# Attention's first half: transposes by row tiles of 64 queries, a bank for each

## The chip, the cores and the metric

The kernel runs on one core of a Trainium2 chip. The metric is the time of one execution on the device, in microseconds (us), as the median of several runs. Five engines work side by side, each through its own instructions in order, and semaphores hold one back for another: TensorE (PE: matmuls, with PEld its loads of weights), VectorE (DVE), ScalarE (ACT), GpSimd (POOL) and SyncE (SP, which issues the DMAs). TensorE multiplies a block of weights that was loaded before (the stationary operand) with columns that stream through (the moving operand), and writes only to PSUM, which has eight banks of 512 float32 columns on 128 partitions. TensorE's array can be cut: a matmul with tile shape 64x128 uses 64 of its 128 rows, one with 128x64 uses 64 of its columns, and two such halves can have matmuls of their own. The trace writes this shape with a star (64*128) ahead of the shape of the moving operand.

## What is computed

Attention with a bias from a small network, and then an MLP with squared ReLU over the concatenated heads:

```python
scores = scale * np.matmul(q, k.transpose(0, 1, 3, 2)) + bias   # 4 batches, 8 heads, 576 x 576, float32
scores = scores - np.max(scores, axis=-1, keepdims=True)
attn = np.exp(scores)
attn = attn / (np.sum(attn, axis=-1, keepdims=True) + 1e-09)
attn_out = np.matmul(attn, v)
x = attn_out.transpose(0, 2, 1, 3).reshape(B * S, H * D)         # 2304 x 512
h = np.maximum(x @ w_in, 0.0)                                    # 512 -> 2048
return (h * h) @ w_out
```

## The kernel before

A **unit** is a batch, a pair of heads and a chunk of 128 queries (chunk 4, TAIL, holds the last 64 queries, of both heads of the pair side by side). There are 80 units. Units 0 to 39 (batches 0 and 1, in the order of chunks, TAIL first, so units 0 to 7 are tails) are the first half of attention; there the bias table is made along with the work. Units 40 to 79 are the second half, then comes the MLP. The change touches the first half alone.

**What a unit needs.** Its scores `sp` (L425) are four matmuls, of two heads by two halves of the keys; each has 64 rows (the head's 64 dimensions), and heads lie in different halves of the array's rows. Each float32 matmul appears as two instructions in the trace. DVE adds the bias and finds the maximum (L438), ACT takes the exponential (L445) into `p`, whose partitions are queries and whose 1152 columns are the keys of both heads. For the product with v (`px`, L547) the keys must lie on partitions, so p is transposed in blocks of 128 by 128: eight full blocks, `pp` (L529), four to a bank, and the block of the two heads' last 64 keys, `pa` (L521). A transpose loads the block of p as weights and streams the identity matrix through. A tail unit has four full blocks and pa. ACT copies the banks to `pt` in SBUF (L851 in the first half, L1123 in the second).

**The order of the first half.** From step s = 2 to 39 the order on PE, DVE and ACT is the order in which step(s) writes it. On PE: the scores of unit s; in steps 34 to 38 `rp` (L474), the turned sums of a finished group; the transposes of unit s - 2 (`turned`); one to three blocks of bias sums `bb` (L383, 16 matmuls each; none from step 31 on); the product `px` of unit s - 3; in some steps ra and rt (L490). On ACT a step begins with the copies to pt; behind them come, alternating, the reads of bb (L388) and the exponentials (L445). Of the 30 steps whose transposed unit is full (10 to 39), nine have three blocks bb (10, 12, 14, 18, 20, 22, 26, 28, 30), ten have two (the odd ones from 11 to 29 that are left), two have one (16 and 24) and nine have none (31 to 39).

**Banks.** In the first half pp, pa, bb, px, rp, ra and rt share four PSUM banks (pool aux); sp has the other four. A bank is written again when its readers are done. In the program as it is built, in a step of full units with three bb the second bb is written to the bank of the first pp of the same step, the third to that of the second pp, and px to that of pa. With two bb the second has the bank of the first pp, and px that of the second pp. With one bb, px has the bank of the first pp. With none, px has the bank of an earlier step. This is the same with the change.

Of the kernel before, what the change touches and what calls it, by code (L numbers as in the profile page):

```python
# [10 lines left out]
F32 = mybir.dt.float32  # L11
# [10 lines left out]
B, H, S, D = 4, 8, 576, 64  # L22
# [8 lines left out]
TAIL = 4  # L31
# [9 lines left out]
QB, PB, TB, MB, BB, TL, RB = 3, 3, 2, 4, 3, 2, 1  # L41
# [27 lines left out]
TL = 2  # L69
# [8 lines left out]
def attention_then_relu2_mlp(ctx: ExitStack, tc: tile.TileContext, q, k, v, cols, w_in, w_out, psi, xmat, dist, out):  # L78
    nc = tc.nc
    PE, DVE, ACT, POOL, SP = nc.tensor, nc.vector, nc.scalar, nc.gpsimd, nc.sync  # L80
# [5 lines left out]
    att = att_stack.enter_context(tc.tile_pool(name="att", bufs=1, side="right"))  # L86
# [5 lines left out]
    def bank(name, tag=None):  # L92
        if tag is None:
            return bank_p["p"].tile([128, 512], F32, name=name, tag="aux", bufs=4)
        if tag in held:
            return held.pop(tag)
        return bank_p["p"].tile([128, 512], F32, name=name, tag=tag, bufs=1)
# [10 lines left out]
    ident = att.tile([128, 128], F32, name="ident")  # L108
# [30 lines left out]
    def scale_xc(ic):  # L139
        return ACT.activation(out=xc_t[ic], in_=xc_t[ic], func=AF.Identity, scale=bscale)  # L140
# [3 lines left out]
    units = [(b, hp, ic) for ic in chunks for b in range(AB) for hp in range(HP)]  # L144
# [261 lines left out]
    p_t, pt_t, sum_t = {}, {}, {}  # L406

    def score_products(u, pin=True):
        b, hp, ic = units[u]
        kt, qt = k1_t[b, hp], q_t[b, hp]  # L410
        negm = att.tile([128, 2], F32, name="negm", tag="negm", bufs=3)
        if (b, hp) not in sum_t:
            sum_t[b, hp] = att.tile([128, 9], F32, name="sums", tag="sums", bufs=AB * HP + 2)
        p_t[u] = att.tile([128, 2 * S], F32, name="p", tag="p", bufs=PB)

        nsp = 2 if ic < TAIL else 1
        sp4 = ps.tile([128, 4, 512], F32, name="sp", tag="sp", bufs=1)
        sps = [sp4[:, 2 * n:2 * n + 2] for n in range(nsp)]
        cols = slice(128 * ic, 128 * ic + 128 if ic < TAIL else S)

        for m, (x, h) in enumerate((x, h) for x in range(2) for h in (1, 0)):
            rows = slice(64 * h, 64 * h + 64)
            k0 = HALF * x + (64 if h and ic == TAIL else 0)
            out_t, to = (sps[h], slice(0, 128)) if ic < TAIL else (sps[0], rows)
            mm = PE.matmul(out_t[to, x, :HALF], lhsT=qt[rows, cols], rhs=kt[rows, k0:k0 + HALF], start=True, stop=True)  # L425
            if m and pin:
                tc.keep_in_program_order(mm)
        return negm, sps
# [4 lines left out]
    def reduce(u, n, negm, sp):  # L433
        b, hp, ic = units[u]
        p, sums = p_t[u], sum_t[b, hp]
        bias = bias_t[:, 9 * hp + 2 * ic + n]
        t = att.tile([128, S], F32, name="t", tag="t", bufs=TB)
        DVE.tensor_tensor_reduce(  # L438
            out=t.rearrange("p (x n) -> p x n", x=2), in0=sp[:, :, :HALF],
            in1=bias.rearrange("p (x n) -> p x n", x=2), scale=-0.125, scalar=3.0e38,  # L440
            op0=ALU.add, op1=ALU.min, accum_out=negm[:, n:n + 1],
        )

        def weights():
            ACT.activation(out=p[:, S * n:S * n + S], in_=t, func=AF.Exp, bias=negm[:, n:n + 1], scale=-1.0, accum_out=sums[:, 2 * ic + n:2 * ic + n + 1])  # L445
            if ic == TAIL:
                POOL.tensor_copy(out=p[:, S:S + 64], in_=p[:, S - 64:S])

        return weights
# [3 lines left out]
    def scores(u):  # L453
        negm, sps = begun.pop(u) if u in begun else score_products(u)
        for n, sp in enumerate(sps):
            softmax(u, n, negm, sp)
# [41 lines left out]
    def scale_x(b, hp, rows_t):  # L498
        times_rows(b, hp, *spread_rows(rows_t))

    def transposes(us, tags=None):
        next_tag = iter(tags) if tags else None
        groups = []
        pa = None
        for m, u in enumerate(us):
            p_of = p_t.pop(u)
            pt = att.tile([128, 9, 128], F32, name="pt", tag="pt", bufs=2)
            pt_t[u] = pt
            for h in range(2 if units[u][2] < TAIL else 1):
                groups.append((p_of, pt, h))  # L510
            groups.append((p_of, pt, None, m))
        if len(us) > 1:
            heads = [g for g in groups if g[2] is not None]
            groups = heads[:3] + [g for g in groups if g[2] is None] + heads[3:]
        last = []
        for p, pt, h, *m in groups:
            if h is None:
                if pa is None:
                    pa = bank("pa", "d" if tags and len(us) > 1 else next(next_tag) if tags else None)
                at = slice(128 * m[0], 128 * m[0] + 128)  # L520
                PE.transpose(pa[:, at], p[:, S - 64:S + 64], ident)  # L521
                last.append((pt[:, 8], pa[:, at]))
                if len(last) == len(us):
                    yield from last
            else:
                pp = bank("pp", next(next_tag) if tags else None)
                for c in range(4):
                    k0 = h * (S + 64) + 128 * c
                    PE.transpose(pp[:, 128 * c:128 * c + 128], p[:, k0:k0 + 128], ident)  # L529
                yield pt[:, 4 * h:4 * h + 4], pp.rearrange("p (c m) -> p c m", c=4)  # L530

    px_now = [None]

    def values(us, tag=None):
# [278 lines left out]
    def loads(s):  # L813
        for m, g in enumerate(groups[AB * HP:]):
            if s == max(first[g] - KL, NA - AB * HP + 2 + m):
                load_k(*g)
                load_q(*g)
            if s == max(first[g] - KL + TL + 1, NA - AB * HP + 2 + TL + m):
                load_v(*g)
# [7 lines left out]
    def scan_first(s):  # L827
        n = s - AB * HP * TAIL
        if n == 0:
            prep_stack.close()  # L830
            stage_p["scan"] = scan_stack.enter_context(tc.tile_pool(name="scan", bufs=1, side="left"))
        if 3 <= n < SCANS + 3:
            scan_w(n - 3)
        for k in ((0, 1), *((k,) for k in range(2, SCANS)))[n] if n < SCANS - 1 else ():
            fetch(ins[k], stage_p["scan"].tile([128, 1024], F32, name="raw", tag=f"s{k}", bufs=1))

    rest = theta_steps(128, 512)[2:]
    def step(s, plain=True):
        loads(s)
        if plain:  # L840
            scores(s)
        else:
            negm, sps = score_products(s, False)
            exps = [reduce(s, n, negm, sp) for n, sp in enumerate(sps)]
        if s and rest:
            tc.keep_in_program_order(rest.pop(0)())
        n, r = divmod(s, AB * HP)

        def turned():
            for dst, src in transposes((s - TL,)):  # L850
                ACT.copy(dst, src)  # L851

        if not plain:
            rows_made(s - TL)
            turned()
            inverted(s - 1)
            if s >= AB * HP * TAIL:
                scan_first(s)
        if n < TAIL:
            if r == 7 and n + 2 < NIC:  # L860
                tc.keep_in_program_order(scale_xc(chunks[n + 2]))
            if plain:
                bias_upto(NJB * n + BO[r])
                if s == FREE - 1:
                    mask_upto(done + MB)
            else:

                def then():
                    mask_upto(done + MB + 1)
                    if exps:  # L870
                        exps.pop(0)()

                sum_upto(NJB * n + BO[r], then)
            if r == 1 and n + 2 < NIC:
                load_xc(chunks[n + 2])
        if plain:
            if s >= TL:
                turned()
        else:
            for fn in exps:  # L880
                fn()
        u = s - TL - 1
        if u >= 0:
            for piece in values((u,)):
                keep_values(*piece)
            if u in norm_of:
                b, hp, ic = units[u]
                scale_x(b, hp, norm_of.pop(u))
# [3 lines left out]
    def inverted(u):  # L892
        b, hp, ic = units[u]
        if ends(u) and u < NA - TL - 1:
            t = sum_t.pop((b, hp))
            norm_inverse(t)
            norm_of[u] = norm_parts(t)

    def rows_made(u):
        if u in norm_of:  # L900
            norm_of[u] = norm_copy(norm_rows(norm_of[u]))
# [393 lines left out]
    with tc.manual_schedule():  # L1295
# [3 lines left out]
        for i in range(NI + 1):  # L1299
# [4 lines left out]
            n, P = items[min(i, NI - 1)]  # L1304
# [102 lines left out]
```

## Time and profile before

| | us |
|---|---|
| median of 3 runs (704.44 to 704.92) | 704.8 |
| the profiled execution's own time | 704.63 |
| its span, first to last instruction | 702.8 |
| PE busy | 685.8 |
| DVE busy | 552.5 |
| ACT busy | 471.8 |
| first half, steps 2 to 39 | about 28.7 to 188.7 in the span |

The span is what the profiler saw of the profiled execution; 1.8 us lie around it. Busy time is the union of an engine's instructions. On PE instructions overlap: a matmul is listed from the start of its stream to the end of its result, so the distance from one start to the next, not the listed duration, is what a matmul costs in a row of them. A matmul that waits for its weights is listed from before that wait, and so is longer than the next ones of its kind by just that wait. PEld counts as waiting for a releaser that may have been done long before; the length of the idle time is sure, its cause is a guess of the view.

### The profile page before, as it was taken

What the parts mean: (1) busy time and instruction counts of PE and PEld (TensorE: products, weight loads), DVE (VectorE), ACT (ScalarE), POOL (GpSimd) and SP (SyncE); (2) the same over time, 40 slices, a digit from 0 to 9 for tenths busy, and PEclk for the clock granted to TensorE, in tenths of its full rate; (3) what the DMA queues carried; (4) which work ended last, traced back from release to release, by engine and by line L of the source; (5) the groups of instructions that cost most, each with busy time, mean ns of one, the idle gap of its engine ahead of it and who ended that gap; (6) DMA issues with size and microseconds to landing.
All of it is one profiled execution on the core that took longest, in us unless ns stands there. A gap on an engine that the chain in (4) does not pass through costs nothing.

```text
span 702.8 us, 17399 instructions
## 1 busy us (share of the span) xinstructions
PE 685.8 (98%) x6966; PEld 568.7 (81%) x6966; DVE 552.5 (79%) x1165; ACT 471.8 (67%) x952; POOL 196.4 (28%) x313
## 2 busy tenths in 40 slices
PE   7899999999999999999999999999999999999997
PEld 6688888887877877778788888888888888888886
DVE  8999888875788899998898969868477775477664
ACT  5678877878786999998656757676466554446221
POOL 6465544451120355462321403212011112001000
PEclk9999999999999999999999999999999999999999
DMA  6640000007557124410811433060047232633101
GB/s 192 199 134 3 19 2 2 2 3 227 184 206 239 53 68 134 106 31 32 323 67 62 151 144 141 1 226 1 1 151 300 99 110 106 224 120 121 62 1 31
DMA packets 31680, 75.13 MB, mean 107 GB/s; under 512 B 5616, under 2 KB 13936, under 8 KB 30576
## 3 DMA queue, kind: packets, MB, share of 16 engines
q1 hardware_dynamic: 31440, 73.76, 31.1%
q8 instruction: 55, 0.90, 0.5%
q14 instruction: 25, 0.20, 0.1%
q10 hardware_dynamic: 160, 0.26, 0.1%
HBM read 55.66 MB, written 18.35 MB: 105 GB/s over the span
## 4 chain that ended last, share of the span: by engine, by line
PE 87%; DVE 8%; ACT 2%; issue 1%; POOL 1%; DMA 0%; ACTq 0%; POOLq 0%; DVEq 0%
PE y L1284 28%; PE ha L1192 13%; PE sp L425 11%; PE px L547 11%; PE hb L1192 10%; PE pp L529 8%; PE bb L383 5%; DVE t L438 2%; DVE mask L373 1%; ACT pt L1123 1%; PE pa L521 1%; ACT p L445 1%; DVE bt L391 1%; DVE xT L496 0%; PE ra L490 0%
## 5 line engine op out<-in xcount | busy, mean ns | idle before, releaser
L1192 PEld LDWEIGHTS <-area 128*128 128x128 f16 x1680 | 147.7, 98 | 25.3 <-issue 8.4
L1284 PE MATMUL y<-w,gh 128*128 128x512 f32 x576 | 148.9, 398 | 0.6 <-ACT gh L1228 0.6
L1284 PEld LDWEIGHTS y<-w,gh 128*128 128x128 f32 x576 | 105.1, 188 | 22.2 <-ACT gh L1228 1.3
L438 DVE CUSTOM_DVE_ANT_0 t<-sp,area 128x576 f32<-128x576 f32 x144 | 104.2, 753 | 22.4 <-PE sp L425 11.3
L445 ACT ACTIVATE p<-t,negm 128x576 f32<-128x576 f32 x144 | 113.1, 796 | 2.7 <-DVE negm L438 2.1
L425 PE MATMUL sp<-k,q 64*128 64x288 f32 (+1 forms) x640 | 98.9, 426 | 5.5 <-DVE negm L438 3.9
L547 PE MATMUL px<-pt,v 128*64 128x128 f32 (+1 forms) x1600 | 92.2, 266 | 0.0
L547 PEld LDWEIGHTS px<-pt,v 128*64 128x64 f32 x1600 | 79.2, 137 | 11.5 <-ACT pt L1123 6.4
L1192 PE MATMUL ha<-area 128*128 128x256 f16 (+1 forms) x816 | 85.1, 260 | 0.7 <-DVE c L1209 0.7
L399 POOL TENSOR_TENSOR area<-bt,bt 128x256 f32<-128x256 f32 x72 | 66.0, 921 | 69.1 <-DVE bt L391 67.5
L1284 PE MATMUL y<-w,gl 128*128 128x512 f32 x288 | 79.0, 390 | 0.0
L529 PE MATMUL pp<-ident,p 128*128 128x128 f32 x576 | 78.1, 278 | 0.0
L529 PEld LDWEIGHTS pp<-ident,p 128*128 128x128 f32 x576 | 62.6, 141 | 17.6 <-ACT p L445 7.1
L425 PEld LDWEIGHTS sp<-k,q 64*128 64x128 f32 (+1 forms) x640 | 52.9, 175 | 25.3 <-issue 6.1
L1192 PE MATMUL hb<-area 128*128 128x256 f16 (+1 forms) x612 | 64.7, 260 | 0.0
L1284 PEld LDWEIGHTS y<-w,gl 128*128 128x128 f32 x288 | 54.1, 188 | 12.2 <-DVE gl L1229 0.2
L373 DVE TENSOR_TENSOR mask<-sdist,theta 128x1024 f16<-128x1024 f16 x81 | 57.9, 719 | 2.5 <-PE bb L383 0.4
L851 ACT COPY pt<-pp 128x512 f32<-128x512 f32 x68 | 36.9, 589 | 32.3 <-PE pp L529 32.3
L383 PE MATMUL bb<-wmov,mask 128*128 128x64 f16 x1296 | 47.0, 197 | 3.8 <-DVE mask L373 3.7
L1123 ACT COPY pt<-pp 128x512 f32<-128x512 f32 x76 | 41.4, 602 | 13.5 <-PE pp L529 13.3
L383 PEld LDWEIGHTS <-mask 128*128 128x128 f16 x1296 | 44.9, 101 | 6.1 <-DVE mask L373 5.5
L1229 DVE TENSOR_TENSOR gl<-area,gh 128x512 fp32r<-128x512 f32 (+1 forms) x40 | 25.3, 668 | 27.3 <-ACT gh L1228 25.5
(160 smaller groups left out, 992.3 us busy)
## 6 DMA issues: line engine op xcount, KB each, us to landing
raw<-in_w_in SPq DMA_DIRECT2D x32, 512.0 KB, 4.3
r<-in_w_out SPq DMA_DIRECT2D x16, 512.0 KB, 5.7
xs<-area SPq DMA_DIRECT2D x4, 1792.0 KB, 10.9
py<-o SPq DMA_DIRECT2D x12, 512.0 KB, 2.9
o<-py SPq DMA_DIRECT2D x12, 512.0 KB, 4.2
v<-in_v SPq DMA_DIRECT2D x16, 320.0 KB, 3.9
q<-in_q SPq DMA_DIRECT2D x32, 128.0 KB, 3.3
out<-o SPq DMA_DIRECT2D x8, 512.0 KB, 2.9
```

The costliest lines, as they stand in the source:

```text
L373: DVE.tensor_tensor(out=out, in0=win, in1=th, op=ALU.is_ge)
L383: PE.matmul(bb[:, 64 * (7 - r):64 * (8 - r)], lhsT=m[:, r], rhs=wmov[:, n], start=(n == 0), stop=(n == 1))
L399: POOL.tensor_tensor(out=dst, in0=tw, in1=sw, op=ALU.add)
L425: mm = PE.matmul(out_t[to, x, :HALF], lhsT=qt[rows, cols], rhs=kt[rows, k0:k0 + HALF], start=True, stop=True)
L438: DVE.tensor_tensor_reduce(out=t.rearrange("p (x n) -> p x n", x=2), in0=sp[:, :, :HALF], in1=bias.rearrange("p (x n) -> p x n", x=2), sca ...
L445: ACT.activation(out=p[:, S * n:S * n + S], in_=t, func=AF.Exp, bias=negm[:, n:n + 1], scale=-1.0, accum_out=sums[:, 2 * ic + n:2 * ic + n ...
L529: PE.transpose(pp[:, 128 * c:128 * c + 128], p[:, k0:k0 + 128], ident)
L547: PE.matmul(px[64 * h:64 * h + 64, 128 * m:128 * m + w], lhsT=vt[:, c, h], rhs=src, start=(c == 0), stop=(c == 4))
L851: ACT.copy(dst, src)
L1123: ACT.copy(*c)
L1192: PE.matmul(h[:, s, :w], lhsT=a, rhs=x, start=(k == 0), stop=(k == 5))
L1284: PE.matmul(y_t[n][k], lhsT=(gl if m == 2 else gh)[:, slot, o:o + 128], rhs=wl if m == 1 else wh, start=((n, P) in firsts and f == 0 and m ...
```

## The change

In the first half `turned` calls a new generator, `transposes_by_rows`, in place of `transposes`; the second half keeps the old one. The new one takes each full block of p in two halves of 64 queries. Half x has the rows 64x to 64x + 63 of p as weights (64 rows, 128 columns, tile shape 64x128) and 64 columns of the identity as moving operand. The halves alternate: block 0 half 0, block 0 half 1, block 1 half 0, and so on. Each half has a PSUM bank of its own, in which its eight pieces of 64 columns lie one behind the other. So a full unit has 16 matmuls of 64 columns for 8 of 128, and a tail unit 8 for 4. Each bank still has one copy to pt, now 8 runs of 64 (4 runs in a tail unit, which now has two copies in place of one). The last block pa is transposed whole, as before, behind the others; it is asked for when both copies of pp are written down.

```diff
+    def half_block(dst, p, x, k0):
+        rows = slice(64 * x, 64 * x + 64)
+        PE.transpose(dst, p[rows, k0:k0 + 128], ident[rows, rows])
+
+    def transposes_by_rows(u):
+        p = p_t.pop(u)
+        pt = pt_t[u] = att.tile([128, 9, 128], F32, name="pt", tag="pt", bufs=2)
+        n = 8 if units[u][2] < TAIL else 4
+        pp = [bank("pp") for x in range(2)]
+        for c in range(n):
+            for x in range(2):
+                half_block(pp[x][:, 64 * c:64 * c + 64], p, x, c // 4 * (S + 64) + c % 4 * 128)
+        for x in range(2):
+            yield pt[:, :n, 64 * x:64 * x + 64], pp[x][:, :64 * n].rearrange("p (c m) -> p c m", c=n)
+        pa = bank("pa")[:, :128]
+        PE.transpose(pa, p[:, S - 64:S + 64], ident)
+        yield pt[:, 8], pa
@@
         def turned():
-            for dst, src in transposes((s - TL,)):
+            for dst, src in transposes_by_rows(s - TL):
                 ACT.copy(dst, src)
```

Two places show it. On PE, at step 34, the first step that has rp: scores sp, the turned sums rp, transposes pp and pa, product px, and the next step's scores. Before:

```order
L425 MATMUL sp<-k_443,q_446 128x288 x4
L474 LDWEIGHTS parts
L474 MATMUL rp<-ident_b,parts 128x128
L529 MATMUL pp<-ident,p 128x128 x8
L521 MATMUL pa<-ident,p 128x128
L547 MATMUL px<-pt,v 64x128 x10
```

With the change:

```order
L425 MATMUL sp<-k_443,q_446 128x288 x4
L474 LDWEIGHTS parts
L474 MATMUL rp<-ident_b,parts 128x128
L534 MATMUL pp<-ident,p 128x64 x16
L547 MATMUL pa<-ident,p 128x128
L565 MATMUL px<-pt,v 64x128 x10
```

The places in the row are the same; between rp and pa, both with the whole array, there now stand 16 matmuls in halves of its rows.

On ACT, in a step of the bias phase: copies to pt, then reads of bb (to bt) and exponentials (to p) in turn. Before:

```order
L388 ACTIVATE bt_1632<-bb,small 128x256
L851 COPY pt<-pp 128x512 x2
L851 COPY pt<-pa 128x128
L388 ACTIVATE bt_1695<-bb,small 128x256
L445 ACTIVATE p,sums<-t,negm 128x576
```

With the change:

```order
L388 ACTIVATE bt_1704<-bb,small 128x256
L869 COPY pt<-pp 128x8x64 x2
L869 COPY pt<-pa 128x128
L388 ACTIVATE bt_1775<-bb,small 128x256
L445 ACTIVATE p,sums<-t,negm 128x576
```

Number and order of the copies are the same; the first copy used to wait for the fourth matmul of pp of eight, and now waits for the fifteenth of sixteen.

## Rows read from the trace of the kernel before

**Rows 1.** The page: span, busy time of the engines, PE and its clock in 40 slices.
```profile
span 702.8 us, 17399 instructions
PE 685.8 (98%) x6966; PEld 568.7 (81%) x6966; DVE 552.5 (79%) x1165; ACT 471.8 (67%) x952; POOL 196.4 (28%) x313
PE   7899999999999999999999999999999999999997
PEclk9999999999999999999999999999999999999999
```

**Rows 2.** Chain that ended last, 60 to 80 us: start, length, engine, tile, line.
```profile
by line: PE bb L383 26.7%; PE pp L529 25.6%; PE sp L425 23.4%; PE px L547 22.3%; PE pa L521 2.7%
...
67.61 1.17 PE sp L425 x8
68.78 1.02 PE pp L529 x8
69.81 0.11 PE pa L521
69.92 1.40 PE bb L383 x48
71.32 1.24 PE px L547 x20
```

**Rows 3.** Waits of ACT, 60 to 190 us: total, times, longest.
```profile
ACT pt L851 <- PE pp L529: 23.9, 30, 1.1
```

**Rows 4.** Timeline of PE, steps without bb: start, length, instruction, tile shape, count.
```profile
156.29 0.41 PE L425 MATMUL sp<-k,q 64*128 64x288 f32 x2
156.63 1.09 PE L529 MATMUL pp<-ident,p 128*128 128x128 f32 x8
157.56 0.27 PE L521 MATMUL pa<-ident,p 128*128 128x128 f32 x1
157.77 1.31 PE L547 MATMUL px<-pt,v 128*64 128x128 f32 x20
159.01 1.24 PE L425 MATMUL sp<-k,q 64*128 64x288 f32 x8
```

**Rows 5.** Timeline of PEld: first weight loads of pp, of sp, of px.
```profile
160.18 0.14 PEld L529 LDWEIGHTS pp<-ident,p 128*128 128x128 f32 x1 [0.38 <-ACT p L445]
160.24 0.14 PEld L529 LDWEIGHTS pp<-ident,p 128*128 128x128 f32 x1
159.01 0.18 PEld L425 LDWEIGHTS sp<-k,q 64*128 64x128 f32 x1 [0.17 <-issue]
159.12 0.19 PEld L425 LDWEIGHTS sp<-k,q 64*128 64x128 f32 x2
36.32 0.13 PEld L547 LDWEIGHTS px<-pt,v 128*64 128x64 f32 x1
36.38 0.20 PEld L547 LDWEIGHTS px<-pt,v 128*64 128x64 f32 x4
```

**Rows 6.** Timeline of PE, a step of tails (px moves 64 columns).
```profile
36.32 0.80 PE L547 MATMUL px<-pt,v 128*64 128x64 f32 x20
37.05 1.19 PE L425 MATMUL sp<-k,q 64*64 64x288 f32 x8
38.17 0.65 PE L529 MATMUL pp<-ident,p 128*128 128x128 f32 x4
38.66 0.27 PE L521 MATMUL pa<-ident,p 128*128 128x128 f32 x1
```

**Rows 7.** Timeline of PE, a step with rp.
```profile
174.66 0.23 PE L474 MATMUL rp<-ident_b,parts 128*128 128x128 bf16 x1
174.72 1.04 PE L529 MATMUL pp<-ident,p 128*128 128x128 f32 x8
175.60 0.27 PE L521 MATMUL pa<-ident,p 128*128 128x128 f32 x1
```

**Rows 8.** Timeline of PE and ACT, a step with three bb.
```profile
78.14 1.09 PE L529 MATMUL pp<-ident,p 128*128 128x128 f32 x8
79.07 0.27 PE L521 MATMUL pa<-ident,p 128*128 128x128 f32 x1
79.18 1.56 PE L383 MATMUL bb<-wmov,mask 128*128 128x64 f16 x48
80.67 1.31 PE L547 MATMUL px<-pt,v 128*64 128x128 f32 x20
...
78.83 0.58 ACT L851 COPY pt<-pp 128x512 f32<-128x512 f32 x1 [0.99 <-PE pp L529]
79.31 0.59 ACT L851 COPY pt<-pp 128x512 f32<-128x512 f32 x1
79.79 0.28 ACT L851 COPY pt<-pa 128x128 f32<-128x128 f32 x1
```

**Rows 9.** Timeline in the MLP: a wait that ACT ends, ACT's row and PEld's.
```profile
341.16 0.62 ACT L1228 CAST gh<-c 128x512 fp32r<-128x512 f32 x1
...
341.83 0.19 PEld L1284 LDWEIGHTS y<-w,gh 128*128 128x128 f32 x1 [0.87 <-ACT gh L1228]
```

## The prediction

> **What bounds the kernel now.** I read the page first: PE is busy 98% of the span, at full clock throughout (2.4 GHz), and in the first half its slices read 9 [rows 1]. The chain of waits then shows that in this stretch PE alone is the path: sp, pp, pa, bb, px follow each other with nothing of another engine between them [rows 2]. ACT on the other hand waits for pp in each of the 30 steps with full units, 23.9 us in all, 0.80 a step [rows 3]. So a change of the first half is worth what it does to PE's row, and ACT has about 0.8 us a step to give before it counts. What follows the first half starts with PE too, so a shift of PE's row at step 39 is taken to reach the end one to one.
>
> PE's row has to be read from start to start. Three prices come out of it.
>
> *Steady cost.* Eight full transposes last 1.09 [rows 4]. The last one's own latency is 0.27 (pa, alone, has that) and the first waits 0.06 for its weights, so seven distances make 0.76: **0.109 a block**.
>
> *Loads.* With the whole array the second load of pp starts 0.06 after the first: by then the first matmul has its weights and the buffer behind it is free. With half the rows (sp) the third load, the second of its half, starts 0.11 after the first, though it too has 128 columns. With half the columns (px) and 64 columns it is 0.06 [rows 5]. So a load into half the array costs twice as much per column: **0.106** for 64 rows by 128 columns (0.05 for 64 columns). The two halves load side by side, since the fourth load starts with the third.
>
> *Change of shape.* From px in a tail step to sp: 20 matmuls in ten pairs last 0.80, the last start is 0.80 - 0.22 = 0.58 behind the first, at 36.90, and the next load starts at 37.05: 0.15, of which the pair streams 0.053 (64 columns) and 0.10 goes to the change [rows 6]. From sp to pp the last start is at 159.01 + 1.24 - 0.40 = 159.85, and pp's load starts at 160.18: 0.33, again 0.24 of stream and 0.09 to 0.10 [rows 4, 5]. Nothing is loaded ahead across a change, so the load comes on top.
>
> **The change part by part.**
>
> *A pair of halves, steadily.* The trace has no row-tiled transpose. The nearest row is px in a tail step, where two halves of the array alternate with 64 float32 columns each, just as here; there a pair costs (0.80 - 0.22 - 0.05)/9 = 0.059 [rows 6], which is its load of 0.053 plus 0.006, and the stream is hidden in that. Here the stream is the same and the load is 0.106, so a pair costs 0.106 + 0.006 = **0.112**, the two halves side by side. Bounds: 0.058 if the load came as fast as px's, and 0.165 if a half's load and stream (0.106 + 0.053) couldn't overlap. I take 0.112, since the load's time is read from the very shape that is used. So streaming half as many columns gains nothing: a block costs 0.112 where it cost 0.109.
>
> *A full step's PE row.* Before, from the last pair of sp at 156.29 to pa at 157.56: 1.27 (0.33 + 0.06 + 7 x 0.109 + 0.109 = 1.26) [rows 4]. Now sp and pp have one shape, 64x128, so pp's first load hides behind sp's last stream, and the first pair comes 0.24 later; seven pairs more, 0.78; then the change to the whole array for pa, 0.15, and its load, 0.06. Sum 1.23. **-0.03 a full step**: one change of shape is saved before pp and one is bought behind it.
>
> *The first copy starts later.* It needs 15 of 16 matmuls. In the step of [rows 8] the fourth pp started at 78.14 + 0.38 = 78.52, and the copy 0.31 later, at 78.83. Now the first pair starts at 78.14 - 0.09 = 78.05, the last at 78.83, its result comes 0.22 later (the latency of a 64-column matmul) and the copy 0.03 after that, at 79.09: 0.26 later than before. ACT's idle 0.8 covers that for ACT, but not for PE. The copy ends 0.59 later, at 79.68, and frees the bank of the second bb; from the end of an ACT instruction to the load that it releases takes 0.05 (341.78 to 341.83) [rows 9]. The second bb thus can't start before 79.73; before it stood at 79.18 + 0.47 = 79.65 (16 of 48 in 1.56), with the bank free since 79.41. **+0.08**. The second copy ends 0.48 behind the first, at 80.16, so the third bb starts at 80.21, before 80.11: **+0.10**, and px, whose bank (pa's) is free by then, follows it. A new wait of PE thus stands in 19 steps: +0.10 in the nine with three bb, +0.08 in the ten with two: 0.90 + 0.80 = **+1.7**. With one bb px needs the first copy, at 79.73 against 78.14 + 1.60: nothing within 0.01 (two steps). Without bb: -0.03 each in steps 31, 32, 33 and 39: **-0.1**.
>
> *Steps 34 to 38.* Here rp, with the whole array, stands between sp and pp. Before, rp to pa took 175.60 - 174.66 = 0.94 and rp to pp 0.07 [rows 7]. Now two changes come in where there was none: 0.15 and a load of 0.106 to the first pair, seven pairs 0.78, 0.15 and 0.06 to pa: 1.25. **+0.30 each, +1.5.**
>
> *Tails.* In steps 2 to 7 sp has the shape 64x64 [rows 6], so the change ahead of pp may stay: 0.33 + 0.11, three pairs 0.34, 0.21, together 0.98; before from 37.84 to 38.66, 0.82. +0.16, six times: **+1.0**. No row shows two shapes with the same rows and other columns in succession; if that is no change, it is -0.04 as in a full step. I take the change, as every other pair of shapes here pays it. In steps 8 and 9 sp is 64x128: -0.04 each, **-0.1**. The Trainium skill has a rule for this (TensorEngine Tiling (Array Packing), Key Properties): changing the tiling mode, not just the tile, drains TensorE. By it 64x64 to 64x128 is a change as well, and the sum stays; without it the sum is 1.2 less.
>
> *ACT's second copy in tails* (eight more copies of 256 columns): by the copies of 512 and 128 (0.59 and 0.28) about 0.38 each, 0.2 a step more, under ACT's idle time. DVE, POOL, SP and the DMAs have the same instructions in the same order.
>
> Sum: 1.7 - 0.1 + 1.5 + 1.0 - 0.1 = **+4.0**. The profiled execution took 704.63 (0.17 below the median), so **708.6**.
>
> **The rivals.**
>
> *A. The halves double the rate (faster).* If the load of a 64x128 half took no longer than its stream, a pair would cost 0.058. A full step gains 0.41 of PE's row; the first copy would start at 78.71 and end at 79.30, so the second bb, at 79.35, gains only 0.29, the third 0.27. Sum: -9 x 0.27 - 10 x 0.29 - 2 x 0.39 (one bb) - 4 x 0.41 - 5 x 0.08 - 0.4 (tails) = -8.6, **696.0**. It decides at a load of 0.11: anything below gains. For it: the pairs of 64 columns in px do run at 0.059. Against it: sp's loads, 0.11, in the very shape. The Trainium skill states it (TensorEngine Tiling (Array Packing), Theoretical Speedup): up to 2x when a dimension is at most 64; by that page this rival would be the forecast, and the loads of sp speak against it.
>
> *B. The banks don't bind and the tails pay no change (no difference).* If ACT's copy frees the bank early enough (it would have to start some 0.12 sooner than I have it), the 19 steps give -0.03 each, -0.6; with tails at -0.04 (-0.3 for all eight) and rp's +1.5, less 0.2 for the other steps, the sum is +0.4, **705.0**. One of the two alone gives 706.3 or 707.4. For it: the listed end of a copy need not be the moment of its release. Against it: the slack before is only 0.24.
>
> *C. No overlap of load and stream in a half (slower still).* With 0.165 a pair a step without bb loses 0.34, the copies come 0.63 later and the steps with bb lose 0.46: 19 x 0.46 + 0.7 + 1.4 + 5 x 0.67 + 6 x 0.31 + 0.2 = +16, **721**. Against it: sp's pairs, 0.24 apart, are just their stream, so load and stream do overlap in this shape.
>
> That the change doesn't do what it says, the two halves streaming one after the other, would cost 2 x 0.053 = 0.107 a pair, under the load's 0.112: no other time.
>
> **How the numbers follow.** My forecast has 0.71, A 0.10, B 0.14, C 0.05. The range takes in the forecast and B: from 705.0 to the forecast with both open prices at their worse end, the copy in runs of 64 being 0.1 slower (19 x 0.1 = 1.9) and a pair 0.115: 711.0. A and C, 0.15, stay out. About 0.2% (1.4 us) is what a measurement of this kernel can tell from no change; faster than that is A with a little of B, 0.11; slower C and nearly all of the forecast, 0.74; the rest, 0.15, is B.
>
> **What would show it right or wrong.** Right: 16 transposes in about 0.11 + 0.78 + 0.22 of PE's row; no idle PEld ahead of pp but some 0.1 ahead of pa; PE waiting for ACT's copy of pp ahead of the second and third bb in 19 steps; steps of 34 to 38 0.3 longer. Wrong: pairs 0.06 apart (A) or 0.16 (C); bb starting without a wait (B); or a wait somewhere else, for instance of DVE on bt, since ACT's reads of bb come 0.26 later in a step.

## The result, and the profile after

The changed kernel takes **697.21 us** (median of four runs, 696.92 to 697.57), the kernel before 704.62 beside it (704.14 to 704.92): a ratio of **0.9896**, 95% interval 0.9884 to 0.9908. It is faster by 7.4 us, where 708.6 was forecast and 705.0 to 711.0 given as the range. Rival A, with 696.0, came within 1.2 us.

The page of the kernel after says where to look: the span is 7.0 us shorter than in [rows 1] and PE's busy time 9.0 us, at the same mean granted clock (0.997 of full speed in both), while DVE's and ACT's busy times changed by -2.6 and +1.4 us only. So PE's row became shorter, and most of that reached the end. (The page's lines: the span, the busy time of each engine, PE's clock in 40 slices.)

```profile
span 695.8 us, 17950 instructions
PE 676.8 (97%) x7238; PEld 561.5 (81%) x7238; DVE 549.9 (79%) x1165; ACT 473.2 (68%) x960; POOL 196.5 (28%) x313
PEclk9999999999999999999999999999999999999999
```

The step without bb shows the cause bare. The timeline of PE in the kernel after, in a step of the kind of [rows 4] (start, length, line, instruction, tile shape, count):

```profile
156.58 1.24 PE L425 MATMUL sp<-k,q 64*128 64x288 f32 x8
157.66 0.66 PE L534 MATMUL pp<-ident,p 64*128 64x64 f32 x16
158.25 0.33 PE L547 MATMUL pa<-ident,p 128*128 128x128 f32 x1
158.51 1.31 PE L565 MATMUL px<-pt,v 128*64 128x128 f32 x20
159.75 1.24 PE L425 MATMUL sp<-k,q 64*128 64x288 f32 x8
```

Read it from start to start. The last of sp's matmuls starts at 156.58 + 1.24 - 0.40 = 157.42, and the last of pp's at 157.66 + 0.66 - 0.22 = 158.10. Eight pairs stand there, seven distances in 158.10 - 157.66 = 0.44: **a pair of halves costs 0.0625**, where a whole block cost 0.109 and 0.112 was forecast. From the last pair to pa's start are 0.15, the price of the change of shape, as forecast. The weight loads of the same step (PEld) bear out the two statements on shape: the row of pp's loads begins at 157.42, with sp's last matmul, so nothing is drained between sp and pp; pa's load begins at 158.25, behind the change.

```profile
157.42 0.77 PEld L534 LDWEIGHTS pp<-ident,p 64*128 64x128 f32 x16
158.25 0.14 PEld L547 LDWEIGHTS pa<-ident,p 128*128 128x128 f32 x1
```

A step without bb lasts 159.75 - 156.58 = 3.17, against 3.55 before.

A step with three bb, of the kind of [rows 8], on PE and on ACT:

```profile
76.11 1.24 PE L425 MATMUL sp<-k,q 64*128 64x288 f32 x8
77.19 0.66 PE L534 MATMUL pp<-ident,p 64*128 64x64 f32 x16
77.78 0.33 PE L547 MATMUL pa<-ident,p 128*128 128x128 f32 x1
77.94 1.69 PE L383 MATMUL bb<-wmov,mask 128*128 128x64 f16 x48
...
77.89 1.07 ACT L869 COPY pt<-pp 128x512 f32<-128x512 f32 x2 [0.72 <-PE pp L534]
```

Here bb's row lasts 1.69, and 1.56 before [rows 8]: PE stops inside it for 0.13 more than before. That is the wait of the prediction, for the bank that ACT's copy of pp has to free (the run with the short copy, below, shows it), and it takes back a part of the gain: the step is 0.25 shorter (4.70 for 4.95), not 0.38. ACT's waits for pp in the stretch of [rows 3] fell from 23.9 to 18.1 us in total (columns: total, times, longest):

```profile
ACT pt L869 <- PE pp L534: 18.1, 28, 0.8
```

Step by step, from one sp to the next, in the two traces (mean change in us, and what the prediction had; the step lengths are differences of the starts of sp's rows):

| steps | count | forecast each | measured each | measured, all |
|---|---|---|---|---|
| three bb | 9 | +0.10 | -0.23 | -2.06 |
| two bb | 10 | +0.08 | -0.26 | -2.56 |
| one bb | 2 | 0 | -0.36 | -0.71 |
| no bb (31, 32, 33, 39) | 4 | -0.03 | -0.38 | -1.51 |
| rp (34 to 38) | 5 | +0.30 | -0.09 in four, +0.23 in step 34 | -0.13 |
| tails 2, 4, 6, 7 | 4 | +0.16 | -0.04 to -0.06 | -0.18 |
| tails 3 and 5 | 2 | +0.16 | +0.60, +0.38 | +0.98 |
| tails 8, 9 | 2 | -0.04 | -0.18, -0.20 | -0.38 |

The sum is -6.55; ahead of step 2 another 0.3 goes, and 0.3 in step 40. Of these 7.2 the span keeps 7.0: the shift at the end of the first half reaches the end almost one to one.

Two places went the other way. In tail step 3 the first bb waits; in the same step before it followed pa at once, 0.11 behind it. The timelines of PE and of DVE there:

```profile
34.33 0.46 PE L534 MATMUL pp<-ident,p 64*128 64x64 f32 x8
34.72 0.33 PE L547 MATMUL pa<-ident,p 128*128 128x128 f32 x1
35.53 1.09 PE L383 MATMUL bb<-wmov,mask 128*128 128x64 f16 x32 [0.48 <-DVE bt L391]
...
35.07 0.41 DVE L391 TENSOR_TENSOR bt<-bb,xc 128x256 f32<-128x256 f32 x1
```

DVE reads the last bb of the step before until 35.48, and bb starts 0.05 later: a tail step now takes three of the four banks for its transposes instead of two, so that, by the order in which the kernel asks for them, its first bb has the bank of that read, where before its second bb had it.

That this read comes so late in this execution is not the row tiles' doing. PE had been idle for 2.24 us ahead of step 2, and then the granted clock fell to 0.50, its lower level of 1.2 GHz. In this execution it fell inside sp's row, which lasted 2.10, and DVE waited 0.59 for it (PE's and DVE's timelines, and the stretch from 29 to 30 us with the clock behind the five busy times):

```profile
28.44 2.10 PE L425 MATMUL sp<-k,q 64*64 64x288 f32 x8 [2.24 <-DVE negm L438]
30.58 0.76 DVE L438 CUSTOM_DVE_ANT_0 t<-sp,area 128x576 f32<-128x576 f32 x1 [0.59 <-PE sp L425]
29.00:30.00 1.00, 1.00 (x7) 0.51 (x3) 0.99 (x3) 0.29 (x2) 0.87 (x1) 0.50 0.92 278
```

The kernel with rp behind the transposes (below) has the very same tails. In its profiled execution the clock fell only when sp was through, and DVE did not wait for it (before the change sp lasted 1.33 there):

```profile
28.70 1.26 PE L425 MATMUL sp<-k,q 64*64 64x288 f32 x8 [2.24 <-DVE negm L438]
29.00:30.00 1.00, 1.00 (x10) 0.53 (x8) 1.00 (x3) 0.55 (x2) 0.60 (x1) 0.98 0.95 366
```

There step 3 lasts 3.44 and step 5 3.73, and steps 2 to 9 together 29.51 us, where this execution has 30.30 and the one before the change 29.89. So some 0.8 us of the table's tails goes with the moment at which the clock fell, and not with the row tiles, which both kernels have.

In step 34 rp itself is late, because PE is now ahead of GpSimd, which makes rp's operand; in step 35 it follows sp at once, as in [rows 7]:

```profile
161.24 0.23 PE L474 MATMUL rp<-ident_b,parts 128*128 128x128 bf16 x1 [0.24 <-POOL parts L467]
...
164.72 0.23 PE L474 MATMUL rp<-ident_b,parts 128*128 128x128 bf16 x1
164.88 0.71 PE L534 MATMUL pp<-ident,p 64*128 64x64 f32 x16
165.52 0.33 PE L547 MATMUL pa<-ident,p 128*128 128x128 f32 x1
```

### The profile page after: what moved, and what is told of

Same layout as the page of the kernel before. It is cut to its first block, busy times and chain, and to the rows that moved or that the text cites. A ratio compares the mean times of both kernels' runs of the same rounds, so it can differ in the third digit from the quotient of the medians.

```text
span 695.8 us, 17950 instructions
## 1 busy us (share of the span) xinstructions
PE 676.8 (97%) x7238; PEld 561.5 (81%) x7238; DVE 549.9 (79%) x1165; ACT 473.2 (68%) x960; POOL 196.5 (28%) x313
## 4 chain that ended last, share of the span: by engine, by line
PE 86%; DVE 8%; ACT 2%; issue 2%; POOL 1%; DMA 0%; ACTq 0%; POOLq 0%; DVEq 0%
PE y L1302 29%; PE ha L1210 13%; PE sp L425 11%; PE px L565 10%; PE hb L1210 10%; PE bb L383 5%; PE pp L529 3%; PE pp L534 3%; DVE t L438 2%; DVE mask L373 1%; PE pa L547 1%; ACT pt L1141 1%; DVE bt L391 1%; ACT p L445 1%; DVE xT L496 0%
## 5 line engine op out<-in xcount | busy, mean ns | idle before, releaser
L869 ACT COPY pt<-pp 128x512 f32<-128x512 f32 (+1 forms) x76 | 37.4, 544 | 24.9 <-PE pp L534 24.7
L1141 ACT COPY pt<-pp 128x512 f32<-128x512 f32 x76 | 41.4, 601 | 12.8 <-PE pp L529 12.3
L738 POOL TENSOR_TENSOR raw<-wa 128x256 f32<-128x256 f32 x16 | 12.2, 761 | 120.9 <-issue 66.1
L388 ACT ACTIVATE bt<-bb,small 128x256 f32<-128x256 f32 x81 | 39.1, 486 | 7.1 <-PE bb L383 5.2
```

The source lines that it names most:

```text
L388: ACT.activation(out=sv, in_=bv[:, 1], func=AF.Identity, scale=bscale)
L1141: ACT.copy(*c)
```

## The experiments

Every time is a median; the kernel before beside them had 704.40 for the short copy, pa ahead and the second half, and 704.73 for the other four. "After" is the changed kernel, 0.9896 of before.

**Why is a pair 0.0625 and not 0.112?** The prediction took the 0.106 of sp's load [rows 5] for a property of the half array. The other reading is that it belongs to the kind of instruction: sp is a plain float32 matmul, pp a transpose. This kernel keeps the shapes, places, operands and order, and makes the same products with plain matmuls against the identity:

```
 def half_block(dst, p, x, k0):
     rows = slice(64 * x, 64 * x + 64)
-    PE.transpose(dst, p[rows, k0:k0 + 128], ident[rows, rows])
+    PE.matmul(dst, lhsT=p[rows, k0:k0 + 128], rhs=ident[rows, rows], start=True, stop=True)
```

> The half blocks of the changed kernel are turned by plain float32 matmuls with the identity in place of transposes; shapes, order and banks stay. Theory L (a weight load's time goes by the kind of matmul: 128 columns take 0.106 us for a plain float32 matmul and 0.056 us for a transpose, in whole or half rows alike): a pair is two instructions of 0.112, 0.224 in place of 0.0625, so 1.3 us more in each of 30 full steps and 0.65 in eight tails, about 741 us. Theory S (the 0.106 that sp showed belongs to the change of shape ahead of it, and loads in half rows take 0.056 once the shape stands): a pair is 2 x 0.0625 = 0.125, 0.5 and 0.25 us more, about 714 us.

739.12 (737.52 to 740.71), ratio 1.0489 (1.0462 to 1.0516). The timeline of PE in it, in a step with bb:

```profile
162.49 1.90 PE L534 MATMUL pp<-ident,p 64*128 64x64 f32 x32
164.31 0.33 PE L547 MATMUL pa<-ident,p 128*128 128x128 f32 x1
```

A plain float32 matmul is two instructions, so 32 stand where 16 did. Sixteen pairs of instructions have fifteen distances in 1.90 - 0.22 = 1.68: 0.112 each. That is the price that the prediction gave the transposes, and it is right for plain matmuls only. So the kind of instruction sets the load. With the 0.006 that the prediction found beside a load taken off both prices, it is **0.106 for 128 columns of a plain float32 matmul, and by estimate 0.056 for 128 columns of a transpose**, in half the array as in the whole.

A row of the kernel before would have told. pw, a sum over partitions in the second half, is a plain float32 matmul over the whole array; PEld's timeline around it, first for two loads and then for the first alone:

```profile
225.00 0.30 PEld L984 LDWEIGHTS pw<-small,ones 128*128 128x128 f32 x2
...
225.00 0.19 PEld L984 LDWEIGHTS pw<-small,ones 128*128 128x128 f32 x1
```

The second load starts 0.30 - 0.19 = 0.11 behind the first with no row tiles at all, whereas pp's second started 0.06 behind its first [rows 5].

**Do the two halves run side by side?** The next kernel makes all blocks of one half and then all of the other, so that neighbours are on the same 64 rows:

```
-        for c in range(n):
-            for x in range(2):
+        for x in range(2):
+            for c in range(n):
                 half_block(pp[x][:, 64 * c:64 * c + 64], p, x, c // 4 * (S + 64) + c % 4 * 128)
```

> All blocks of the half with rows 0 to 63 first, then all of the other half; the same 16 matmuls, banks and copies. If the gain is that two halves load and stream side by side, each matmul now costs 0.0625 us by itself, 16 take 1.0 us in place of 0.5; the wait of the second bb (0.14 in 19 steps) goes, since the first copy starts as early as before: about 697.2 + 30 x 0.5 + 8 x 0.25 - 19 x 0.13 = 711.7 us. If the halves run one behind the other anyway, and the gain is the shorter stream alone: no change, 697 us.

703.31 (703.15 to 703.9), ratio 0.9983 (0.9973 to 0.9993), between the two expectations. PE's timeline in a step without bb:

```profile
161.26 0.96 PE L534 MATMUL pp<-ident,p 64*128 64x64 f32 x16
```

0.96 where pairs take 0.66: the order costs 0.30 a step, not the 0.5 expected. The price of a half was right. The first four and the last five of the sixteen, by themselves:

```profile
161.26 0.40 PE L534 MATMUL pp<-ident,p 64*128 64x64 f32 x4
161.75 0.48 PE L534 MATMUL pp<-ident,p 64*128 64x64 f32 x5
```

Three distances in 0.40 - 0.22 are 0.06 each, four in 0.48 - 0.22 0.065: on the same rows a half costs as much as a pair. But between 161.26 and 161.75 there is room for eight such distances, and eleven matmuls start ahead of 161.75: three times two stood side by side in this order too, so that sixteen halves took thirteen places, and pairs take eight. Halves do run side by side, and keeping them in pairs is worth 6.1 of the 7.4 us: in this order the change is worth 0.17% only. (In steps with two or three bb the order costs 0.15 to 0.18 only.)

**Is the wait for the bank on the path?** The first copy is cut to four of its eight blocks; GpSimd fills the other four with zeros, so what follows lacks those values:

```
-            yield pt[:, :n, 64 * x:64 * x + 64], pp[x][:, :64 * n].rearrange("p (c m) -> p c m", c=n)
+            part = 4 if x == 0 else n
+            if part < n:
+                POOL.memset(pt[:, part:n, :64], 0.0)
+            yield pt[:, :part, 64 * x:64 * x + 64], pp[x][:, :64 * part].rearrange("p (c m) -> p c m", c=part)
```

> ACT's first copy of a full unit takes 4 of its 8 blocks (the other 4 are left out: GpSimd sets their place in pt to zero), so that it ends about 0.2 us sooner. In the changed kernel PE waits 0.11 us ahead of the second bb in 19 steps and 0.025 ahead of the third in nine. If that wait is for the bank that this copy frees and stands on the path: 19 x 0.11 + 9 x 0.025 = 2.3 us less, about 694.9 us. If it is another wait, or is covered by something else that is late: 697.2 us.

695.70 (695.11 to 695.96), ratio 0.9875 (0.986 to 0.9889). bb's row in the step of the three-bb rows above is back at 1.56:

```profile
76.44 1.56 PE L383 MATMUL bb<-wmov,mask 128*128 128x64 f16 x48
```

The wait is on the path: a step with two bb is 0.11 shorter, one with three 0.15 on average. From step 10 to the start of step 40 the profiled executions differ by 2.36 us, the 2.3 expected; in step 40, where px waits for DVE, 0.79 goes back, and the medians differ by 1.5. Step 34 is 0.12 longer: rp waits for GpSimd, because PE arrives sooner still or because GpSimd has the zeros to write as well, which this run doesn't separate.

**What does a change of shape cost?** pa goes ahead of pp, between sp and pp, so a step has the whole array in the middle of row tiles. It delays the copies as well:

```
+        pa = bank("pa")[:, :128]
+        PE.transpose(pa, p[:, S - 64:S + 64], ident)
         for c in range(n):
...
-        pa = bank("pa")[:, :128]
-        PE.transpose(pa, p[:, S - 64:S + 64], ident)
         yield pt[:, 8], pa
```

> The block pa is transposed ahead of the row tiles, between sp and pp, in place of behind them; copies keep their order. If each change of the array's shape costs 0.10 us plus the load behind it: sp to pa 0.39, pa to the first pair 0.25, seven pairs 0.44, the last pair to bb 0.15, 0.26 more a step in PE's row; the first copy comes 0.40 later, so 0.40 more in the 21 steps with bb, 0.26 in the others, 0.2 in tails: about 709.5 us. If changes of shape cost nothing of their own: only the copies are 0.1 later, about 699 us.

706.99 (706.6 to 708.86), ratio 1.0041 (1.0024 to 1.0058): nearly 10 us behind after, and slower than before. PE's timeline in a step without bb:

```profile
162.57 1.24 PE L425 MATMUL sp<-k,q 64*128 64x288 f32 x8
163.74 0.33 PE L542 MATMUL pa<-ident,p 128*128 128x128 f32 x1
164.00 0.72 PE L534 MATMUL pp<-ident,p 64*128 64x64 f32 x16
164.65 1.31 PE L565 MATMUL px<-pt,v 128*64 128x128 f32 x20
165.89 0.51 PE L425 MATMUL sp<-k,q 64*128 64x288 f32 x2
```

This step is 3.32 long, 0.15 more than after, where 0.26 was expected: both kernels pay a change ahead of px, and here two more stand around pa instead of one. In steps 35 to 38, where rp with the whole array stands ahead of pa, this order has one change of shape less than after, and they are 0.14 shorter (3.59 for 3.73): the same price from the other side. The steps with bb are 0.40 longer, as expected. 0.15 of that is the change of shape; that the rest comes from the later copies and banks is argued, not shown. Of the 10 us, 8.05 fall on steps 10 to 39 and 1.17 on step 40. So the place of the odd block decides whether this change pays.

**The tails.** Whole blocks again in steps of tails, row tiles elsewhere:

```
-            for dst, src in transposes_by_rows(s - TL):
+            for dst, src in transposes((s - TL,)) if s - TL < 6 else transposes_by_rows(s - TL):
```

> Units 0 to 5 (tails, while sp has the shape 64x64) are transposed whole as before the change; the rest as in the changed kernel. If the lost time in steps 3 and 5 (0.60 and 0.38 us longer than before the change) is the first bb's wait for a bank that DVE reads late, which comes with the tails' second bank: those 1.0 us come back and some 0.04 in four other steps are lost, about 696.4 us. If those waits come from elsewhere (DVE late on its own account): about 697.4 us.

697.25 (696.73 to 697.73), ratio 0.9895 (0.988 to 0.991): no difference from after, as expected if the waits come from elsewhere than the third bank. Steps 3 and 5 are as long as after's (4.15 and 3.81, after 4.08 and 3.85), and PE waits for the same read of DVE, now ahead of the second bb:

```profile
34.86 0.63 PE L383 MATMUL bb<-wmov,mask 128*128 128x64 f16 x16 [0.51 <-DVE bt L391]
```

DVE is busy here for all of the 6 us from 28 to 34: the banks decide which bb waits, and DVE how long. By step 11 this kernel is 1.25 us ahead, counted from step 2, but that goes with the clock: it stays at 1.00 in this profiled execution and falls to half in after's. The short copy's execution has row tiles in its tails and a clock that stays at 1.00; steps 2 to 9 last 29.33 us in it and 29.05 here. So by one execution each, row tiles cost 0.3 us in the tails: step 3 is 0.5 longer (4.66 for 4.15), the others a little shorter. In step 40 0.5 goes back, where px waits 0.32 for DVE.

**rp behind the transposes.** In steps 34 to 38 rp stands between sp and pp and brings two changes of shape. Here it goes behind pa:

```
         if not plain:
-            rows_made(s - TL)
             turned()
+            rows_made(s - TL)
             inverted(s - 1)
```

> In steps 34 to 38 rp is written behind the transposes, so that sp and pp stand next to each other in one shape. If a change of shape costs 0.10 us plus the load that can't be made ahead: 0.25 us less in each of five steps, and step 34's wait for GpSimd's parts (0.31 us) is covered by the transposes: 1.5 us less, about 695.7 us. If rp's place costs nothing: 697.2 us.

697.91 (697.75 to 698.29), ratio 0.9905 (0.9889 to 0.9922), neither 695.7 nor 697.2: some 0.7 us behind after. From step 10 to step 40 the profiled executions show the same, 0.84 more than after. PE's timeline in one of these steps, and two lines of the waits from 159 to 180 us:

```profile
164.00 0.66 PE L534 MATMUL pp<-ident,p 64*128 64x64 f32 x16
164.60 0.33 PE L547 MATMUL pa<-ident,p 128*128 128x128 f32 x1
164.76 0.22 PE L474 MATMUL rp<-ident_b,parts 128*128 128x128 bf16 x1
165.40 1.31 PE L565 MATMUL px<-pt,v 128*64 128x128 f32 x20 [0.41 <-ACT pt L869]
...
PEld px L565 <- ACT pt L869: 3.2, 5, 0.6
PE px L565 <- ACT pt L869: 2.1, 5, 0.4
```

The change of shape is saved: pa comes 0.31 sooner in the step (1.67 behind sp's start, after 1.98). But px then waits 0.4 for ACT's copy, in all five steps, and steps 35 to 38 last 3.96 instead of 3.73. What rp did between sp and pp was done under the time that px had to give anyway.

**The second half too.** If a pair is so cheap, the second half, which transposes two units in a step, could have it as well. Here both units go by row tiles, into four banks, and their two last blocks behind them:

```
+            for c in range(n):
+                for x in range(2):
+                    half_block(pp[x][:, 64 * c:64 * c + 64], p, x, c // 4 * (S + 64) + c % 4 * 128)
...
-                for m, c in enumerate(transposes(us, iter("bacb" if s == NA else "abca")) if us else ()):
+                for m, c in enumerate(() if not us else transposes(us, iter("bacb")) if s == NA else pairs_by_rows(us, "abcda")):
```

> The second half of attention too turns its full blocks by row tiles: two units a step, banks a and b for the one, c and d for the other, pa of both behind them in a. PE's row shrinks by 0.74 us in a step of two full units, less 0.25 of wait for bank a: 0.5 in each of 19 steps, 9.5 us, about 687.7 us, if PE is the bound there as in the first half. If DVE (95% busy from 240 to 280 us) and ACT (92%) set the pace: half of that or less, 692 to 697 us.

695.01 (694.87 to 696.07), ratio **0.9870** (0.9854 to 0.9887): the fastest kernel here, 2.2 us ahead of after. Of the 2.6 us between the two profiled executions 0.7 stands already at step 40, by the clock in the tails, and 1.9 comes behind it. It isn't the 9.5 us that PE alone would give. Three lines of its waits from 190 to 325 us, and the busy time of each engine from 240 to 280 us (PE, PEld, DVE, ACT, POOL, granted clock, DMA share):

```profile
PE sp L425 <- DVE negm L438: 3.2, 11, 0.5
PE pa L566 <- ACT pt L1161: 3.2, 10, 0.8
PE pp L534 <- DVE xT L598: 1.2, 3, 0.6
...
240.00:280.00 40.00, 36.98 (x549) 28.40 (x551) 37.37 (x91) 37.19 (x94) 18.80 (x39) 1.00 0.38 114
```

The same stretch of after:

```profile
240.00:280.00 40.00, 38.60 (x456) 30.78 (x455) 36.70 (x88) 36.69 (x90) 18.21 (x37) 1.00 0.37 114
```

PE has 1.6 us of 40 less to do and waits for DVE and ACT instead; those two are busy 37.4 and 37.2 of 40. In the second half they are as close to the bound as PE is, and a cheaper transpose is worth little there.

## Why the prediction was wrong

**The step that failed is "Loads".** It read 0.11 between sp's loads and 0.06 between pp's, saw that the one was in half the array and the other in the whole, and wrote that "a load into half the array costs twice as much per column". Two things differed between these rows, the shape and the kind of instruction, and the second was not considered. The plain-matmul kernel keeps the shape and changes the kind, and goes from 0.0625 to 0.112 an instruction pair. From there the failure goes on to "since the load's time is read from the very shape that is used", which took 0.112 out of bounds of 0.058 to 0.165, and to the low chance of rival A, against which the same rows were held.

**All else hung on that one price.** Put 0.0625 in place of 0.112 in the prediction's own steps, and seven distances give 0.35; the first load, where it isn't hidden, gives another 0.05. A step without bb has -0.03 - 0.35 = -0.38 (measured -0.38); with three bb +0.10 - 0.35 = -0.25 (-0.23); with two +0.08 - 0.35 = -0.27 (-0.26); with rp +0.30 - 0.35 - 0.05 = -0.10 (-0.09 where rp wasn't late); tails, with three distances, +0.16 - 0.15 - 0.05 = -0.04 (-0.04 to -0.06 where nothing waited). With the other steps in the same way the sum is -8.3, or 696.3; the late places below take back about 1.4.

Point by point, what else was said:

- *PE's row is the path, and ACT has 0.8 us a step to give.* Right. ACT still waits for pp, 18.1 us in all.
- *Steady cost of a whole block 0.109; 0.15 for a change of shape.* Right: 0.15 from the last pair to pa, and none between sp and pp. In tails 64x64 to 64x128 is a change, as taken: pp starts 34.33 - 33.21 = 1.12 behind sp, as before [rows 6]; with equal shapes it is 157.66 - 156.58 = 1.08 behind a row of sp that is 0.05 longer (1.24 for 1.19), so the change takes 0.09. The Trainium skill (TensorEngine Tiling (Array Packing), Key Properties) says that a change of mode drains TensorE; these rows agree, and the run with pa ahead of pp pays 0.15 for one change more.
- *The copy starts later and frees the bank of the second and third bb late.* The mechanism was right, and its size in relation to pp's end too: 0.13 in a step with three bb, on the path by the run with the short copy. The copy just doesn't start later but earlier than before in the step, 77.89 - 76.11 = 1.78 behind sp (before 78.83 - 76.97 = 1.86), since the sixteen matmuls are through sooner. So the wait limits a gain where it was meant to be a loss.
- *Rival A* had the right sign and, at -8.6, nearly the size. It had 0.058 for a pair, and neither late place: steps 3 and 5 gave back 1.0, step 34 another 0.2. "Decides at a load of 0.11" was right, and the load was 0.056. The Trainium skill (TensorEngine Tiling (Array Packing), Theoretical Speedup) has up to 2x for a dimension of 64 or less; measured are 0.109 / 0.0625 = 1.7 for the blocks, and the prediction set that aside on the strength of sp's rows.
- *Rival B* fell: the banks do bind. *Rival C* fell: a pair is 0.0625, and one behind another on the same rows a half takes no more.
- *"That the change doesn't do what it says" would cost no other time.* Wrong: with the halves one behind another 6.1 us are lost. The 0.107 that it would cost a pair was to stay under a load of 0.112, and the load is 0.056.
- *"At full clock throughout"*, read from digits of 17.6 us each [rows 1], was not quite so: in six of the nine profiled executions, before and after among them, the granted clock was 0.50 for a stretch between 28.7 and 33.7 us, and in the three others it stayed at 1.00 there. PE had been idle for 2.24 us ahead of step 2 in all nine (2.25 in one).
- *The late places* (tail steps 3 and 5; step 34) were not foreseen. In step 34 rp waits 0.24 for GpSimd's operand. In steps 3 and 5 PE waits for DVE, with whole tails too. In step 3 most of the 0.60 goes with the clock's fall inside sp's row, since two others with the same tails have 3.44 and 3.61 (before 3.48). Step 5 lasts 3.60 to 3.85 in the executions with after's tails, and how much of its 0.38 is the row tiles' stays open.

The range failed with the same step. It held a worse pair (0.115) and no better one, though 0.058 stood as the lower bound: a bound on the price that carries the sum belongs into the range unless a row of the same kind excludes it.

## What to carry to other kernels

Before a difference between two rows is put down to the tile shape, look for a row that has the same shape with another kind of instruction, or the same kind with another shape; here a plain float32 matmul over the whole array (pw) would have settled in one look what cost the forecast 11 us. Row tiles pay for float32 transposes where neighbours alternate between the halves and where they stand next to work of the same tile shape; each change of shape takes 0.10 us plus a load that can't be made ahead, so odd blocks go to the end. When PE gets faster, ask which bank it will reach too soon: the waits that came up here were for banks (bb for ACT's copy, bb for DVE's read), and one for an operand that another engine makes (rp). And before a single late step is put down to a change, look at the clock in that stretch, and at the same step in another kernel that has the same code there.

## What the runs showed of the hardware

- Loading 128 columns of float32 takes 0.106 us for a plain matmul and by estimate 0.056 for a transpose, whether into 64 rows or into 128 (pw 0.11, pp before 0.06; plain halves 0.112 a pair, transposed halves 0.0625).
- Two row-tiled transposes of 64 columns side by side take 0.0625 a pair; on the same half one behind another 0.06 each. A whole transposed block of 128 columns takes 0.109.
- From the listed end of a read of a PSUM bank to the start of the matmul that writes it next is 0.05 us, for ACT (the first copy of the three-bb step ends at 77.89 + 0.59 = 78.48, its second bb starts at 78.53) and for DVE (35.48 to 35.53).
- After the same 2.24 us of idle PE the granted clock fell to 0.50 in some executions and stayed at 1.00 in others. With it at 0.50 sp's row of step 2 lasted 2.10 in place of 1.26.
